# Decode attention over a key/value cache: the order of key and value loads and of the scores and values products within a slot

## The chip, the cores and the metric

The kernel runs on one core of one Trainium2 chip. The metric is the device time of one execution in microseconds: the median of three runs. A profile of one further execution gives the span from its first to its last instruction, and what each engine did in between. TensorE multiplies matrices (PE in the profile; its weight loads, PEld, are listed apart), VectorE (DVE), ScalarE (ACT) and GpSimd (POOL) do the rest, and SyncE (SP) issues the loads. On-chip data lie in SBUF, the results of products in PSUM.

## What is computed

One decoding step for 8 sequences: a layer norm, attention of 32 query heads over a cache of 8 key/value heads with 8192 positions of 128 elements each, and beside it a small token-mixing block, summed with the input.

```python
B, D, Hq, Hkv, Sk, Dh, F = 8, 512, 32, 8, 8192, 128, 1792
xn = _layernorm(x)                                   # x: (B, 1, D)
q = (xn @ wq).reshape(B, 1, Hq, Dh).transpose(0, 2, 1, 3)
k = repeat(k_cache, Hq // Hkv, axis=1)               # cache: (B, Hkv, Sk, Dh)
v = repeat(v_cache, Hq // Hkv, axis=1)
p = softmax(einsum("bhqd,bhkd->bhqk", q, k) * Dh ** -0.5)
o = einsum("bhqk,bhkd->bhqd", p, v)
a = o.transpose(0, 2, 1, 3).reshape(B, 1, Hq * Dh) @ wo
h = _layernorm(xn)
u = gelu(einsum("bsd,sf->bdf", h, w1) + b1)
y = (einsum("bdf,fs->bds", u, w2) + b2).transpose(0, 2, 1)
return x + a + y
```

All of it is float32. The two caches hold 64 pairs (sequence, key/value head) with 4 MB of keys and 4 MB of values each; with the weights that makes 553.69 MB to be read.

## The kernel before

The work is cut into 64 **slots**, one for each pair (sequence, key/value head), numbered by `s`. `slot` (L365) is called for slots 0 and 1 ahead of a loop, for slots 2 to 61 in a loop of four slots a turn (L408), and for 62 and 63 behind it. There are two buffers for keys, `K[0]` and `K[1]`, and two for values, `V[0]` and `V[1]`; pair `s` uses number `k = s % 2`. The order of the instructions on each engine is written by hand: an engine runs its own in the order of the code, and semaphores hold it where data are missing.

A slot of the kernel before does this, for pair `s` with its keys in `K[k]`:

- DVE transposes the keys in place in four quarters (`turn`, L238), and between the first and the second the probabilities of pair `s - 1`, which lie in PSUM (`sm_turn`, L267).
- PE multiplies the probabilities of pair `s - 1` with its values (`pv`, L274, 16 products for a pair, which the profile counts as 32), sums their denominators (`o_sums`, L295), ends the mixing block's step of the slot before (`mx_end`, L341) and begins a new one (`mx_begin`, L325).
- SP issues the load of the values of pair `s + 1` into `V[1 - k]`, where those of `s - 1` lay.
- PE makes the scores of pair `s` (`qk`, L244, as many products as `pv`); then SP issues the load of the keys of pair `s + 2` into `K[k]`.
- DVE picks the results of pair `s - 1` out of PSUM (`o_pick`, L279 to L282), PE places them (`o_place`, L285).
- ACT and POOL do the mixing block's step (`mx_steps`, L329 to L337), DVE prepares the queries and the mixing block's data of the next slot (`q_place`, `mx_pick`) and adds the mixing block's result (`y_add`, L306).
- Softmax: DVE takes the maximum (`sm_max`, L250); one product spreads it over the partitions and DVE makes the bias of it (`sm_bias`, L254 to L256); ACT takes the exponential (`sm_exp`, L259); DVE scales the results of pair `s - 1` (`o_norm`, L298 to L300); PE brings the probabilities into the order that the next slot's `sm_turn` needs (`sm_place`, L263, the placing product).

All loads of keys, values and the output weights go through SP's queue, in the order of the code. The loop is made with `iteration_sync="staggered"`: each of its four slots is a stage, and the semaphores of a stage are set back while the loop goes on. Line L408 is where the engines' events for that stand. In the code, the calls of `tc.previous_stage_wait` put the point at which PE, DVE, ACT and POOL report the stage before as finished inside the slot; there is none for SP.

Behind slot 63 come the values product of the last pair, its results (`o_last`, L288 to L291), the regrouping of all results (`regroup`, L420 to L422: the first seven sequences ahead of that values product, the last one behind it), and the product with the output weights: 24 of its 32 tiles into one PSUM tile (L436), which is copied out and folded (L439 to L442), and the last eight tiles straight into the sum (L445). `load_wo` (L80) brings these weights into `K[0]` and `K[1]` once the last keys are used, the second half in pieces of 8, 4, 3 and 1 tiles. L446 copies the sum, L447 writes the output.

Of the kernel before, what the change touches and what calls it, by code (L numbers as in the profile page):

```python
# [14 lines left out]
B, D, HQ, HKV, SK, DH, F = 8, 512, 32, 8, 8192, 128, 1792  # L15
REP = HQ // HKV
P = 128
NT = SK // P
Q = 32
NB = P // Q  # L20
NG = NT // 16
NU = NT // NG
BS = Q // B
# [5 lines left out]
N_IT = B * HKV  # L29
NW = 24  # L30
# [4 lines left out]
def attn_mixer_kernel(ctx: ExitStack, tc: tile.TileContext, x, kc, vc, wq, wo, w1, b1, w2, b2, out):  # L35
    nc = tc.nc
# [12 lines left out]
    def misc():  # L49
        turns[0] += 1  # L50
        return MI[turns[0] % 2]
# [5 lines left out]
    V = [ring.tile([P, NT, DH], F32, name=f"v{k}") for k in range(2)]  # L57
# [8 lines left out]
    def load(to, src, n, pieces=(NT,)):  # L66
        rows = src.rearrange("b h (p t) d -> (b h) p t d", p=P)[n]
        at = 0
        for w in pieces:
            nc.sync.dma_start(to[:, at:at + w, :], rows[:, at:at + w, :])  # L70
            at += w
# [4 lines left out]
    def load_wo(a, pieces):  # L76
        rows = wo.rearrange("(p a c) n -> a p c n", p=P, a=2)[a]
        at = 0
        for w in pieces:
            nc.sync.dma_start(WO[a][:, at:at + w, :], rows[:, at:at + w, :])  # L80
            at += w
# [13 lines left out]
    quarter = [slice(j * D // NB, (j + 1) * D // NB) for j in range(NB)]  # L95
# [34 lines left out]
    fold = const.tile([P, Q], F32, name="fold")  # L130
# [19 lines left out]
    OX = const.tile([P, N_IT, REP, NB], F32, name="ox")  # L150
# [14 lines left out]
    xo = const.tile([P, 32, Q], F32, name="xo")  # L165
    nc.vector.memset(xo, 0.0)
    wide = const.tile([P, D], F32, name="wide")
# [4 lines left out]
    O = [ps_o.tile([P, 512], F32, name=f"o{k}") for k in range(2)]  # L172

    MH = ps_h.tile([P, 512], F32, name="mh")
    MI = [ps_m.tile([P, 512], F32, name=f"misc{k}") for k in range(3)]
# [60 lines left out]
    def turn(k, a, w=NT // 4):  # L236
        t = K[k][:, a:a + w, :].rearrange("p t d -> p (t d)")
        nc.vector.transpose(t, t)  # L238

    def qk(k):  # L240
        kt = K[k].rearrange("p (u g) d -> p g u d", g=NG)
        for j in range(NB):
            for g in range(NG):
                nc.tensor.matmul(S[k][g * Q:(g + 1) * Q, :], W[k][:, j, :], kt[:, g, :, j * Q:(j + 1) * Q],  # L244
                                 start=(j == 0), stop=(j == NB - 1))
# [3 lines left out]
    def sm_max(k):  # L249
        nc.vector.tensor_reduce(MR, S[k], AX.X, ALU.max)  # L250
# [7 lines left out]
    def sm_exp(k):  # L258
        nc.scalar.activation(PR[k], S[k], AF.Exp, bias=NBIAS, scale=SCALE, accum_out=LR[:, k:k + 1])  # L259

    def sm_place(k):
        m = misc()
        nc.tensor.matmul(m, perm, PR[k], start=True, stop=True)  # L263
        return m

    def sm_turn(k, m):
        nc.vector.transpose(PT[k], m)  # L267
# [3 lines left out]
    def pv(k, u0=0, u1=NU):  # L271
        for u in range(u0, u1):
            c = u % NB
            nc.tensor.matmul(O[k][c * Q:(c + 1) * Q, :], PT[k][:, u * Q:(u + 1) * Q],  # L274
                             V[k][:, u * NG:(u + 1) * NG, :].rearrange("p t d -> p (t d)"),
                             start=(u < NB), stop=(u >= NU - NB))

    def o_pick(k):
        nc.vector.tensor_tensor(OM.rearrange("p (g d) -> p g d", g=NG), O[k].rearrange("p (g d) -> p g d", g=NG),  # L279
                                dm.unsqueeze(2).to_broadcast([P, NG, DH]), ALU.mult)  # L280
        nc.vector.tensor_add(OB, OM[:, :256], OM[:, 256:])
        nc.vector.tensor_add(OB[:, :DH], OB[:, :DH], OB[:, DH:])  # L282

    def o_place(k):
        nc.tensor.matmul(MH[:, k * REP:(k + 1) * REP], OB[:, :DH], sel, start=True, stop=True)  # L285

    def o_last(k):
        nc.vector.tensor_copy(OM[:, :256], O[k][:, :256])  # L288
        nc.scalar.copy(OM[:, 256:], O[k][:, 256:])
        for g in range(NG):  # L290
            nc.tensor.matmul(MH[:, k * REP:(k + 1) * REP], OM[:, g * DH:(g + 1) * DH], selg[:, g, :],  # L291
                             start=(g == 0), stop=(g == NG - 1))

    def o_sums(k):
        nc.tensor.matmul(MH[:, 64 + k * REP:64 + (k + 1) * REP], LR[:, k:k + 1].to_broadcast([P, P]), sel, start=True, stop=True)  # L295

    def o_norm(k, s):
        nc.vector.reciprocal(RD, MH[:, 64 + k * REP:64 + (k + 1) * REP])  # L298
        nc.vector.tensor_tensor(OS, MH[:, k * REP:(k + 1) * REP], RD, ALU.mult)  # L299
        nc.vector.tensor_tensor(OX[:, s], OS.unsqueeze(2).to_broadcast([P, REP, NB]),  # L300
                                block.unsqueeze(1).to_broadcast([P, REP, NB]), ALU.mult)

    proj, mixed = MH[:, P:2 * P], MH[:, 2 * P:3 * P]

    def y_add():
        nc.vector.tensor_add(yacc, mixed, yacc)  # L306
# [17 lines left out]
    def mx_begin(k):  # L324
        nc.tensor.matmul(MI[2][:FP, :], BM[k].to_broadcast([B, FP]), hn, start=True, stop=True)  # L325

    def mx_steps(k, loop):
        for j in range(NF // HKV):
            nc.scalar.activation(G, MI[2][:FP, :], AF.Gelu_apprx_tanh, bias=MW[k][:, 1, j:j + 1], scale=MW[k][:, 0, j:j + 1])  # L329
            if loop and not j:  # L330
                tc.previous_stage_wait(nc.scalar.engine)
            nc.gpsimd.tensor_tensor(G if j else ACC, G, MW[k][:, 2, j:j + 1].to_broadcast([FP, D]), ALU.mult)  # L332
            if loop and not j:
                tc.previous_stage_wait(nc.gpsimd.engine)
            if j:
                nc.gpsimd.tensor_add(ACC, ACC, G)  # L336
        nc.scalar.activation(sink, epst[:1], AF.Exp)  # L337

    def mx_end(k):
        for j in range(NB):  # L340
            nc.tensor.matmul(mixed[j * Q:(j + 1) * Q, :], BW[k], ACC[:, quarter[j]], start=True, stop=True)  # L341
# [5 lines left out]
    m = misc()  # L347
# [14 lines left out]

    def slot(s, k, placed, left=2, loop=False):  # L365

        if placed is not None:
            turn(k, 0)
            sm_turn(1 - k, placed)
            for a in range(1, 4):  # L370
                turn(k, a * quart)
            pv(1 - k)
            o_sums(1 - k)
            mx_end(1 - k)
        mx_begin(k)
        if loop:
            tc.previous_stage_wait(nc.tensor.engine)
        if left:
            load(V[1 - k], vc, s + 1)
        qk(k)  # L380
        if left > 1:
            load(K[k], kc, s + 2)
        elif left:
            load_wo(0, (NT // REP,))
        else:
            load_wo(1, (NW - 16, 4, 3, 1))
        if placed is not None:
            o_pick(1 - k)
            o_place(1 - k)
        mx_steps(k, loop)  # L390
        if left:
            q_place(s + 1, 1 - k)
            mx_pick(1 - k, s + 1)
        if placed is not None:
            y_add()
        if loop:
            tc.previous_stage_wait(nc.vector.engine)
        sm_max(k)
        sm_bias()
        sm_exp(k)  # L400
        if placed is not None:
            o_norm(1 - k, s - 1)
        return sm_place(k)

    tc.prologue_barrier()
    m = slot(0, 0, None)
    m = slot(1, 1, m)
    with tc.For_i(2, N_IT - 2, 4, iteration_sync="staggered") as s:  # L408
        for n in range(4):
            m = slot(s + n, n % 2, m, loop=True)  # L410
            if n < 3:
                tc.stage_boundary()
    m = slot(N_IT - 2, 0, m, left=1)
    m = slot(N_IT - 1, 1, m, left=0)

    def regroup(b0, b1, copy):
        for b in range(b0, b1):
            nc.tensor.matmul(O[0][:, b * Q:(b + 1) * Q], OX[:, b * HKV:(b + 1) * HKV].rearrange("p h r j -> p (h r j)"), fold,  # L420
                             start=True, stop=True)
        copy(xo.rearrange("p c (b s) -> p c b s", s=BS)[:, :, b0:b1, 0],  # L422
             O[0][:, b0 * Q:b1 * Q].rearrange("p (b c) -> p c b", c=Q))

    sm_turn(1, m)
    regroup(0, B - 1, nc.scalar.copy)
    pv(1)
    o_sums(1)
    mx_end(1)
    o_last(1)  # L430
    o_norm(1, N_IT - 1)
    regroup(B - 1, B, nc.vector.tensor_copy)
    y_add()
    for c in range(NW):
# [3 lines left out]
        nc.tensor.matmul(proj[j * Q:(j + 1) * Q, :], gather[:, j].rearrange("p b s -> p (b s)"), yacc, start=True, stop=False)  # L438
    nc.vector.tensor_copy(wide[:, :256], S[0][:, :256])  # L439
    nc.scalar.copy(wide[:, 256:], S[0][:, 256:])  # L440
    for j in range(NB):
        nc.tensor.matmul(proj[j * Q:(j + 1) * Q, :], fold, wide[:, quarter[j]], start=False, stop=False)  # L442
    for c in range(NW, 32):
        for j in range(NB):
            nc.tensor.matmul(proj[j * Q:(j + 1) * Q, :], xo[:, c, :], WO[1][:, c - 16, quarter[j]], start=False, stop=(c == 31))  # L445
    nc.vector.tensor_copy(yacc, proj)  # L446
# [29 lines left out]
```

## Time and profile before

| | us |
|---|---|
| median of 3 runs (lowest, highest) | 1298.01 (1297.66, 1300.28) |
| the profiled execution's own time | 1300.48 |
| its span | 1298.7 |
| busy: PE, DVE, ACT, POOL | 905.7, 857.5, 331.3, 218.0 |
| mean granted TensorE clock | 0.769 |
| read from memory | 553.69 MB, 426 GB/s over the span |

In the rows that follow, a line such as "604.03 0.33 SPq L70" of the timeline gives the start, the duration, the engine and the line of the kernel, then what was written from what; in square brackets stands how long the engine had been idle and what ended that. A row of a group of instructions gives the busy time of all of them and the mean duration of one in ns, then the idle time before them and what ended most of it. An engine's name with a q behind it is its sequencer: what it does there is not counted as busy. Rows of stretches give, for each stretch of time, the busy time (and the number) of PE, PEld, DVE, ACT and POOL, then the granted clock of TensorE as a share of full speed, the busy share of the DMA engines, and GB/s.

### The profile page before, as it was taken

How to read it: one execution, taken by the hardware profiler on the slowest of the kernel's cores; microseconds unless marked ns; L12 is line 12 of the kernel's file. 1: busy time of each engine (PE TensorE's matmuls, PEld its weight loads, DVE VectorE, ACT ScalarE, POOL GpSimd, SP SyncE). 2: the span in 40 equal slices, each digit the busy share in tenths (PEclk: the TensorE clock that was granted, in tenths of full speed). 3: DMA queues.
4: the chain of work that ended last, by engine and by line, in shares of the span. 5: the costliest groups of instructions: out<-in, count | busy, mean ns of one | idle time of the engine just before them, and what ended most of it. 6: DMA issues, size and time to landing. Idle time of an engine off the chain costs nothing.

```text
span 1298.7 us, 15589 instructions
## 1 busy us (share of the span) xinstructions
PE 905.7 (70%) x5498; PEld 271.0 (21%) x5498; DVE 857.5 (66%) x1261; ACT 331.3 (26%) x458; POOL 218.0 (17%) x205
## 2 busy tenths in 40 slices
PE   4657767767767767766766766776766776776777
PEld 1112212212212212212212211221221221211223
DVE  3666766766766776776776776776676676676671
ACT  1223123223223223223223213213213312312321
POOL 1112122122112112112112112112112212212211
PEclk9678778778768778768777777867777877877877
DMA  9999999999999999999999999999999999999994
GB/s 405 435 433 426 432 435 436 436 432 428 432 436 436 435 432 428 433 436 436 434 432 428 434 436 436 434 432 428 434 436 436 433 429 432 434 436 436 433 427 196
DMA packets 19789, 553.84 MB, mean 426 GB/s; under 512 B 2332, under 2 KB 2364, under 8 KB 2628
## 3 DMA queue, kind: packets, MB, share of 16 engines
q1 hardware_dynamic: 19620, 553.67, 98.8%
q8 instruction: 7, 0.11, 0.0%
q0 software_dynamic: 160, 0.04, 0.0%
q14 instruction: 2, 0.02, 0.0%
HBM read 553.69 MB, written 0.02 MB: 426 GB/s over the span
## 4 chain that ended last, share of the span: by engine, by line
PE 58%; DVE 20%; issue 15%; DMA 6%; DVEq 1%; POOL 0%; ACT 0%; POOLq 0%
PE o L274 28%; PE s L244 17%; DVE k L238 8%; PE misc L325 5%; DMA k<-in_A_k_cache_dram 4%; DVE mr L250 3%; DVE pt L267 3%; DMA v<-in_A_v_cache_dram 3%; PE misc L254 2%; PE mh L341 2%; PE mh L285 2%; PE mh L295 2%; DVE sq L255 1%; DVE nb L256 1%; DVE os L299 1%
## 5 line engine op out<-in xcount | busy, mean ns | idle before, releaser
L238 DVE STREAM_TRANSPOSE k<-k 128x2048 f32<-128x2048 f32 x256 | 574.0, 2280 | 154.5 <-issue 131.2
L274 PE MATMUL o<-v,pt 128*32 128x512 f32 x2048 | 370.3, 889 | 193.3 <-DVE pt L267 191.8
L329 ACT ACT_TABLE_LOAD x64 | 82.1, 1283 | 799.0 <-PE misc L325 787.7
L244 PE MATMUL s<-k,w 128*32 128x512 f32 x2048 | 234.6, 599 | 0.0
L332 POOL TENSOR_TENSOR macc<-g,mw 112x512 f32<-112x512 f32 x64 | 66.7, 1042 | 989.4 <-ACT g L329 989.4
L274 PEld LDWEIGHTS o<-v,pt 128*32 128x32 f32 x2048 | 87.0, 155 | 504.4 <-issue 359.2
L263 PE MATMUL misc<-pr,perm 128*128 128x512 f32 x128 | 116.3, 1006 | 105.6 <-ACT pr L259 105.6
L306 DVE TENSOR_TENSOR yacc<-mh,yacc 128x128 f32<-128x128 f32 x64 | 18.7, 292 | 188.2 <-PE mh L285 188.2
L329 ACT ACTIVATE g<-misc,mw 112x512 f32<-112x512 f32 x128 | 99.5, 777 | 79.3 <-POOL macc L332 77.8
L244 PEld LDWEIGHTS s<-k,w 128*32 128x32 f32 x2048 | 60.2, 110 | 166.4 <-issue 140.9
L337 ACT ACT_TABLE_LOAD x64 | 82.1, 1283 | 1.1
L336 POOL TENSOR_TENSOR macc<-macc,g 112x512 f32<-112x512 f32 x64 | 80.8, 1263 | 5.1
L332 POOL TENSOR_TENSOR g<-g,mw 112x512 f32<-112x512 f32 x64 | 66.6, 1040 | 56.9 <-ACT g L329 56.9
L254 PE MATMUL misc<-nident,mr 128*128 128x128 f32 x128 | 31.2, 326 | 62.7 <-DVE mr L250 62.7
L325 PE MATMUL misc<-hn,bm 8*112 8x512 f32 x128 | 71.7, 640 | 0.6 <-DVE mw L315 0.6
L259 ACT ACTIVATE pr<-s,nb 128x512 f32<-128x512 f32 x64 | 44.0, 687 | 35.1 <-DVE rd L298 23.9
L263 PEld LDWEIGHTS misc<-pr,perm 128*128 128x128 f32 x128 | 25.8, 252 | 117.8 <-ACT pr L259 115.9
L250 DVE TENSOR_REDUCE mr<-s 128x1 f32<-128x512 f32 x64 | 43.6, 681 | 6.6 <-PE s L244 6.6
L267 DVE STREAM_TRANSPOSE pt<-misc 128x512 f32<-128x512 f32 x64 | 43.2, 675 | 2.5 <-PE misc L263 2.5
L279 DVE TENSOR_TENSOR om<-o,dm 128x512 f32<-128x512 f32 x63 | 41.7, 662 | 2.5 <-PE o L274 2.1
L255 DVE TENSOR_TENSOR sq<-misc,hmask 128x128 f32<-128x128 f32 x64 | 18.7, 292 | 37.1 <-PE misc L254 37.1
L254 PEld LDWEIGHTS misc<-nident,mr 128*128 128x128 f32 x128 | 19.0, 187 | 69.1 <-DVE mr L250 69.1
(98 smaller groups left out, 378.3 us busy)
## 6 DMA issues: line engine op xcount, KB each, us to landing
v<-in_A_v_cache_dram SPq DMA_DIRECT2D x64, 4096.0 KB, 19.8
k<-in_A_k_cache_dram SPq DMA_DIRECT2D x63, 4096.0 KB, 24.2
v<-in_A_wq_dram SPq DMA_DIRECT2D x2, 4096.0 KB, 17.0
k<-in_A_k_cache_dram SPq DMA_DIRECT2D x2, 2048.0 KB, 30.3
k<-in_A_wo_dram SPq DMA_DIRECT2D x1, 4096.0 KB, 25.2
k<-in_A_wo_dram SPq DMA_DIRECT2D x1, 2048.0 KB, 10.1
k<-in_A_wo_dram SPq DMA_DIRECT2D x1, 1024.0 KB, 12.2
k<-in_A_wo_dram SPq DMA_DIRECT2D x1, 768.0 KB, 13.5
```

The source lines that it names most:

```text
L238: nc.vector.transpose(t, t)
L244: nc.tensor.matmul(S[k][g * Q:(g + 1) * Q, :], W[k][:, j, :], kt[:, g, :, j * Q:(j + 1) * Q], start=(j == 0), stop=(j == NB - 1))
L250: nc.vector.tensor_reduce(MR, S[k], AX.X, ALU.max)
L254: nc.tensor.matmul(m[:, :P], MR.to_broadcast([P, P]), nident, start=True, stop=True)
L263: nc.tensor.matmul(m, perm, PR[k], start=True, stop=True)
L267: nc.vector.transpose(PT[k], m)
L274: nc.tensor.matmul(O[k][c * Q:(c + 1) * Q, :], PT[k][:, u * Q:(u + 1) * Q], V[k][:, u * NG:(u + 1) * NG, :].rearrange("p t d -> p (t d)"), ...
L325: nc.tensor.matmul(MI[2][:FP, :], BM[k].to_broadcast([B, FP]), hn, start=True, stop=True)
L329: nc.scalar.activation(G, MI[2][:FP, :], AF.Gelu_apprx_tanh, bias=MW[k][:, 1, j:j + 1], scale=MW[k][:, 0, j:j + 1])
L332: nc.gpsimd.tensor_tensor(G if j else ACC, G, MW[k][:, 2, j:j + 1].to_broadcast([FP, D]), ALU.mult)
L336: nc.gpsimd.tensor_add(ACC, ACC, G)
L337: nc.scalar.activation(sink, epst[:1], AF.Exp)
```

## The change

In each slot, SP issues the load of the keys of pair `s + 2` ahead of that of the values of pair `s + 1`; the latter moves to the end of the slot. The scores of pair `s` are made ahead of the values product of pair `s - 1`. That product runs in two halves, one ahead of the placing product of pair `s` and one behind it. Sums, pick, placing and scaling of the results (`o_sums`, `o_pick`, `o_place`, `o_norm`) are those of pair `s - 2` now, so they are a slot later; a new argument `n` of `slot` (0, 1, 2) leaves out in the first two slots what has no pair yet. In the last slot the regrouping of the first seven sequences moves ahead of the scores and into another PSUM tile (`MI[0]`). Behind the last slot the results of pairs 62 and 63 are done one after the other, and the fold products stand behind four of the eight last tiles.

```diff
--- before.py
+++ after.py
@@ -362,72 +362,84 @@
 
 
 
-    def slot(s, k, placed, left=2, loop=False):
-
-        if placed is not None:
+    def slot(s, k, placed, n, left=2, loop=False):
+
+        if n:
             turn(k, 0)
             sm_turn(1 - k, placed)
             for a in range(1, 4):
                 turn(k, a * quart)
-            pv(1 - k)
-            o_sums(1 - k)
+        if n > 1:
+            o_sums(k)
+        if n:
             mx_end(1 - k)
         mx_begin(k)
         if loop:
             tc.previous_stage_wait(nc.tensor.engine)
-        if left:
-            load(V[1 - k], vc, s + 1)
+        if not left:
+            regroup(0, B - 1, nc.scalar.copy)
         qk(k)
         if left > 1:
             load(K[k], kc, s + 2)
-        elif left:
-            load_wo(0, (NT // REP,))
-        else:
+        elif not left:
             load_wo(1, (NW - 16, 4, 3, 1))
-        if placed is not None:
-            o_pick(1 - k)
-            o_place(1 - k)
+        if n > 1:
+            o_pick(k)
+            o_place(k)
         mx_steps(k, loop)
         if left:
             q_place(s + 1, 1 - k)
             mx_pick(1 - k, s + 1)
-        if placed is not None:
+        if n:
             y_add()
         if loop:
             tc.previous_stage_wait(nc.vector.engine)
         sm_max(k)
         sm_bias()
         sm_exp(k)
-        if placed is not None:
-            o_norm(1 - k, s - 1)
-        return sm_place(k)
+        if n:
+            pv(1 - k, 0, NU // 2)
+        if n > 1:
+            o_norm(k, s - 2)
+        m = sm_place(k)
+        if n:
+            pv(1 - k, NU // 2, NU)
+        if left:
+            load(V[1 - k], vc, s + 1)
+        if left == 1:
+            load_wo(0, (NT // REP,))
+        return m
+
+    def regroup(b0, b1, copy):
+        for b in range(b0, b1):
+            nc.tensor.matmul(MI[0][:, b * Q:(b + 1) * Q], OX[:, b * HKV:(b + 1) * HKV].rearrange("p h r j -> p (h r j)"), fold,
+                             start=True, stop=True)
+        copy(xo.rearrange("p c (b s) -> p c b s", s=BS)[:, :, b0:b1, 0],
+             MI[0][:, b0 * Q:b1 * Q].rearrange("p (b c) -> p c b", c=Q))
 
     tc.prologue_barrier()
-    m = slot(0, 0, None)
-    m = slot(1, 1, m)
+    m = slot(0, 0, None, 0)
+    m = slot(1, 1, m, 1)
     with tc.For_i(2, N_IT - 2, 4, iteration_sync="staggered") as s:
         for n in range(4):
-            m = slot(s + n, n % 2, m, loop=True)
+            m = slot(s + n, n % 2, m, 2, loop=True)
             if n < 3:
                 tc.stage_boundary()
-    m = slot(N_IT - 2, 0, m, left=1)
-    m = slot(N_IT - 1, 1, m, left=0)
-
-
-
-    def regroup(b0, b1, copy):
-        for b in range(b0, b1):
-            nc.tensor.matmul(O[0][:, b * Q:(b + 1) * Q], OX[:, b * HKV:(b + 1) * HKV].rearrange("p h r j -> p (h r j)"), fold,
-                             start=True, stop=True)
-        copy(xo.rearrange("p c (b s) -> p c b s", s=BS)[:, :, b0:b1, 0],
-             O[0][:, b0 * Q:b1 * Q].rearrange("p (b c) -> p c b", c=Q))
+    m = slot(N_IT - 2, 0, m, 2, left=1)
+    m = slot(N_IT - 1, 1, m, 2, left=0)
+
+
 
     sm_turn(1, m)
-    regroup(0, B - 1, nc.scalar.copy)
-    pv(1)
+    pv(1, 0, NU // 2)
+    o_pick(0)
+    o_place(0)
+    o_sums(0)
+    o_norm(0, N_IT - 2)
+    pv(1, NU // 2, NU)
     o_sums(1)
+    o_last(1)
     mx_end(1)
-    o_last(1)
     o_norm(1, N_IT - 1)
     regroup(B - 1, B, nc.vector.tensor_copy)
     y_add()
@@ -438,9 +450,10 @@
         nc.tensor.matmul(proj[j * Q:(j + 1) * Q, :], gather[:, j].rearrange("p b s -> p (b s)"), yacc, start=True, stop=False)
     nc.vector.tensor_copy(wide[:, :256], S[0][:, :256])
     nc.scalar.copy(wide[:, 256:], S[0][:, 256:])
-    for j in range(NB):
-        nc.tensor.matmul(proj[j * Q:(j + 1) * Q, :], fold, wide[:, quarter[j]], start=False, stop=False)
     for c in range(NW, 32):
+        if c == NW + 4:
+            for j in range(NB):
+                nc.tensor.matmul(proj[j * Q:(j + 1) * Q, :], fold, wide[:, quarter[j]], start=False, stop=False)
         for j in range(NB):
             nc.tensor.matmul(proj[j * Q:(j + 1) * Q, :], xo[:, c, :], WO[1][:, c - 16, quarter[j]], start=False, stop=(c == 31))
     nc.vector.tensor_copy(yacc, proj)
```

## The prediction

> **What bounds the kernel now.** First the page's head and its queue table, then the busy time by stretches of the loop and of the end.
>
> ```profile
> span 1298.7 us, 15589 instructions
> ...
> q1 hardware_dynamic: 19620, 553.67, 98.8%
> ```
> ```profile
> 91.90:1234.40 1142.50, 807.33 (x4839) 236.71 (x4838) 780.48 (x1121) 300.99 (x413) 197.36 (x177) 0.76 1.00 433
> ```
> ```profile
> 1280.00:1284.00 4.00, 3.86 (x34) 1.82 (x26) 0.53 (x2) 0.37 (x1) 0.00 (x0) 0.83 0.36 146
> ```
>
> The one load queue fills 98.8% of the span, and its share is 1.00 in the loop (the columns are PE, PEld, DVE, ACT, POOL, clock, DMA share, GB/s). Loads end near 1281.4 (0.36 of the 4 us after 1280). So the loop is bound by the transfers, and 17 us of tail follow. One slot in order of time:
>
> ```profile
> 595.54 2.31 DVE L238 STREAM_TRANSPOSE k<-k 128x2048 f32<-128x2048 f32 x1 [1.53 <-issue]
> ...
> 598.37 6.66 DVE L238 STREAM_TRANSPOSE k<-k 128x2048 f32<-128x2048 f32 x3
> ```
> ```profile
> 604.03 0.33 SPq L70 DMA_DIRECT2D v<-in_A_v_cache_dram  x1
> ...
> 605.52 3.64 PE L244 MATMUL s<-k,w 128*32 128x512 f32 x32
> ...
> 609.30 0.33 SPq L70 DMA_DIRECT2D k<-in_A_k_cache_dram  x1
> ...
> 609.72 0.68 DVE L250 TENSOR_REDUCE mr<-s 128x1 f32<-128x512 f32 x1
> ...
> 609.83 1.04 POOL L332 TENSOR_TENSOR g<-g,mw 112x512 f32<-112x512 f32 x1 [0.89 <-ACT g L329]
> ...
> 610.46 0.49 PE L254 MATMUL misc<-nident,mr 128*128 128x128 f32 x2 [0.98 <-DVE mr L250]
> ...
> 611.77 0.69 ACT L259 ACTIVATE pr<-s,nb 128x512 f32<-128x512 f32 x1 [0.50 <-DVE rd L298]
> ...
> 612.60 2.07 PE L263 MATMUL misc<-pr,perm 128*128 128x512 f32 x2 [1.66 <-ACT pr L259]
> 615.02 2.31 DVE L238 STREAM_TRANSPOSE k<-k 128x2048 f32<-128x2048 f32 x1 [2.78 <-issue]
> ...
> 618.08 5.83 PE L274 MATMUL o<-v,pt 128*32 128x512 f32 x32 [3.40 <-DVE pt L267]
> ```
>
> Compute is done before the slot is over: DVE idles 2.78 us before the next transposes. What ends that idleness matters most here. The events of the loop line L408, and the wait of SP's queue on it:
>
> ```profile
> L408 POOLq EVENT_SEMAPHORE  x2: 17/17/17, 614.7 to 614.7; - x2
> L408 DVEq EVENT_SEMAPHORE  x2: 21/21/21, 614.7 to 614.8; - x2
> L408 PEldq EVENT_SEMAPHORE  x2: 51/51/51, 614.7 to 614.8; - x2
> ...
> L408 POOLq COMPARE_BRANCH  x1: 49/49/49, 611.0 to 611.0; - x1
> ...
> L408 SPq EVENT_SEMAPHORE  x1: 28/28/28, 614.6 to 614.6; - x1
> ```
> ```profile
> SPq L408 <- DMA k<-in_A_k_cache_dram: 263.1, 59, 5.4
> ```
>
> POOL had branched to the next slot at 611.0, yet it, DVE and PE all pass L408 only at 614.7, just after SP's event at 614.6. SP stands there, 59 times, until a K load lands. I read it so: **at each slot boundary every engine waits for SP**, and SP gives that release after the last load it issues in the slot, once the loads of the slot before have landed. Now the last issue (K, 609.30) comes 5 us before the landing, so only the landing counts: one slot lasts two transfers.
>
> ```profile
> 91.92 2.31 DVE L238 STREAM_TRANSPOSE k<-k 128x2048 f32<-128x2048 f32 x1 [2.26 <-DMA k<-in_A_k_cache_dram]
> ```
> ```profile
> 1234.47 2.31 DVE L238 STREAM_TRANSPOSE k<-k 128x2048 f32<-128x2048 f32 x1 [1.82 <-issue]
> ```
>
> From slot 3 to slot 62 are 59 slots in 1142.55 us, 19.37 each.
>
> **The change, part by part.** *SP.* K for pair s+2 is issued first (it waits for the scores, as now), then V for s+1, which waits for the second half of the values product, now PE's last work in the slot. Nothing follows it on SP but the release, and behind that stand all four other engines. So the next slot can't begin before the chain transposes, scores, softmax, half, placing product, half, V issue, release has run through; the early key load buys nothing inside the loop, as DVE may not touch the keys before the release. Slots no longer overlap, and the chain is the period:
>
> - release to first transpose 0.2 (estimate from 614.6/614.7 against 615.02, half of that in the slots without a branch); four transposes with the turn of the probabilities between, 595.54 to 605.03: 9.49; to PE 0.1. The results' pick and placing no longer wait for a product of their own slot; DVE does the pick under the scores, as now.
> - scores. They take the place at which the values product now starts after idle time:
>
> ```profile
> L274 PE MATMUL o<-v,pt 128*32 128x512 f32 x2048 | 370.3, 889 | 193.3 <-DVE pt L267 191.8
> ...
> L244 PE MATMUL s<-k,w 128*32 128x512 f32 x2048 | 234.6, 599 | 0.0
> ```
> ```profile
> 47.82 0.69 DVE L250 TENSOR_REDUCE mr<-s 128x1 f32<-128x512 f32 x1 [6.64 <-PE s L244]
> ...
> 50.63 1.12 PE L263 MATMUL misc<-pr,perm 128*128 128x512 f32 x2 [1.58 <-ACT pr L259]
> ```
> ```profile
> 53.33 6.61 PE o L274 x32
> ```
> ```profile
> 609.20:612.50 3.30, 0.77 (x4) 0.48 (x4) 1.90 (x7) 2.77 (x5) 2.30 (x2) 0.97 0.87 377
> 612.50:615.00 2.50, 2.07 (x2) 0.50 (x2) 0.00 (x0) 0.05 (x1) 0.00 (x0) 0.50 1.03 446
> ...
> 618.10:621.00 2.90, 2.90 (x16) 0.87 (x20) 2.90 (x2) 0.00 (x0) 0.00 (x0) 0.50 0.89 384
> ```
>
>   Both products have the same shapes and count; the one at the head of PE's burst takes 370.3/64 = 5.79 us, the one behind it 234.6/64 = 3.67, and the granted clock is 0.50 at the burst's start. After the change PE has only small products at the slot's head and then waits until the transposes end, 9.7 after the release. So scores: 5.79, and the values 3.64 in all (ends: 3.64, and 6.61, the dearest cold one in the chain of waits).
> - end of scores (609.16) to end of the bias product (610.95): 1.79. Then half the values 1.82, under which bias, exponential and normalization lie (the exponential ends at 612.46, 3.3 after the scores; the half ends 3.6 after). Placing product at full clock 1.12, second half 1.82.
> - to SP 0.15 (the K issue at 609.30 follows the scores' end, 609.16, by 0.14), issue 0.33, release 0.1.
>
> Sum 0.2 + 9.49 + 0.1 + 5.79 + 1.79 + 1.82 + 1.12 + 1.82 + 0.15 + 0.33 + 0.1 = **22.7 us a slot**, 3.34 above now. Two transfers take 19.37, so the loads land in time, and the queue stands empty some 3 us a slot. With all at full clock the sum is 20.55; with scores at 6.6, 23.5.
>
> *Mixer.* Its start no longer waits for the values product, so ACT and POOL run beside the transposes.
>
> ```profile
> L332 POOL TENSOR_TENSOR macc<-g,mw 112x512 f32<-112x512 f32 x64 | 66.7, 1042 | 989.4 <-ACT g L329 989.4
> ...
> L336 POOL TENSOR_TENSOR macc<-macc,g 112x512 f32<-112x512 f32 x64 | 80.8, 1263 | 5.1
> ```
>
> No row shows POOL beside a transpose. Bounds: nothing to all of POOL's 1.04 + 1.04 + 1.26 = 3.3 us added to the chain. The nearest: the reduction at 609.72 with POOL running from 609.83 took 0.68, the one at 47.82 with POOL idle 0.69. So I take nothing.
>
> *Head.* K for pair 2 is issued behind the same scores as now; slot 1's values come after its scores, yet their V is issued before the queue is empty. Slot 3 waits for as many bytes as now: no change.
>
> *Tail.* Counted from slot 62's release (about 1234.3 now, so 64.4 to the end). After the change V for 63 is issued at about 22.3. The queue is empty by then, so a startup is paid:
>
> ```profile
> 0.75 0.86 SPq L63 DMA_DIRECT2D v<-in_A_wq_dram  x2
> ```
> ```profile
> 22.78 3.64 PE L207 MATMUL s<-v,sq 128*32 128x512 f32 x32 [2.95 <-DMA v<-in_A_wq_dram]
> ```
>
> Two transfers took 22.0 from an idle queue, 2.7 over 19.37. Three transfers (V, both halves of Wo): 22.3 + 2.7 + 29.1 = 54.1. Pair 63 is barely ahead of that (estimates from the terms above): no release stands behind slot 62, so DVE begins its keys at 18.7; transposes to 28.2, scores to 34, halves and placing of pair 62 to 40.5, the values of 63 to 44.5, its result some 3 later, and then the projection of 24 tiles to 54:
>
> ```profile
> 1285.39 6.70 PE L436 MATMUL s<-k,xo 128*32 128x512 f32 x48 [0.37 <-DVE xo L422]
> ```
>
> Regrouping of the first seven batches (moved under the last transposes) and the fold product (moved past four tiles) leave the path. Behind the last byte:
>
> ```profile
> L445 PE MATMUL mh<-k,xo 128*32 128x128 f32 x64 | 2.1, 273 | 0.0
> ```
> ```profile
> 1295.26 0.29 DVE L446 COPY yacc<-mh 128x128 f32<-128x128 f32 x1 [2.67 <-PE mh L445]
> ```
>
> half of the last 2.1, the copy, and 3.15 to the span's end: 4.5. The tail is 58.6, 5.8 less than now (ends: nothing, and the 12 of the first rival).
>
> Total: 1298.7 + 59 x 3.34 - 5.8 = 1490 of span. The profiled run took 1300.48 for its span of 1298.7, and the median of the runs is 1298.01, 0.7 under that span. Forecast: **1489 us**.
>
> **Rivals.**
>
> 1. *Faster, transfers stay the bound.* If engines can enter the next slot without SP's last issue, the queue stays full, the last byte lands near 1281.4 and 4.5 follow: 1286, 1285 by the median. For it: DVE's own work to the normalization is below 19.37. Against: POOL waiting from 611.0 to 614.7. It decides where the second half ends under 19.37 - 0.6 after the release. 0.07.
> 2. *Slower, but the scores run at full clock* (PE's small products keep it up): 20.55 a slot, 1292.2 + 59 x 1.18 = 1362. Against: the 0.50 rows after a shorter idle time. The Trainium skill, "TensorE: Matmul & The Clock Gate", Part 1, says to model the warm-up as under 1% of a span; by that the scores cost about the same anywhere, and this would be the time. The trace differs: 2.1 us in each of 64 slots, a tenth of the span. 0.04.
> 3. *Slower still*: the clock falls again in the gap after the scores, as it has by 612.5, so that halves and placing run at half rate: 2 x 1.5 + 0.95 more, 26.65 a slot, 1292.2 + 59 x 7.28 = 1722; or POOL takes its 3.3 from the transposes, 26.0 a slot, 1684. Against: the first half now fills that gap. 0.09 in all, partial cases included.
>
> **How the numbers follow.** The forecast has 0.80. 21.8 to 24.1 a slot (PE's phase against its clock, a little of rival 3) gives 1436 to 1572, which holds nearly all of it and some of rival 3: about 8 in 10. A measurement of this kernel tells 0.2% from no change, 2.6 us. Only rival 1 is faster, 0.07; no change needs a slot of 19.4 to 19.5, 0.01; slower 0.92.
>
> **What would show it.** Right: transposes of successive slots start 22.7 apart; SP waits on L70 for the values product and hardly on L408; DMA share in the loop about 0.85 and some 370 GB/s; scores near 5.8 a slot, values near 3.7; L408 events of all engines right behind the V issue. Wrong: a DMA share of 1.00 and slots of 19.4 (rival 1); scores at 3.7 (rival 2); transposes above 2.31 or a clock of 0.50 under the halves (rival 3). The sum falls with the reading of L408 alone: if the release doesn't hang on the V issue, the change gains 1%.

## The result, and the profile after

| | before | after |
|---|---|---|
| median of the runs, us (lowest, highest; runs) | 1299.06 (1297.66, 1300.28; 4) | 1513.37 (1512.55, 1513.92; 4) |
| span of the profiled execution, us (its own time) | 1298.7 (1300.48) | 1511.3 (1513.12) |
| mean granted clock | 0.769 | 0.747 |

The ratio is 1.165, with an interval of 1.1629 to 1.167: the change makes the kernel slower by a sixth. The forecast of 1489 us is 24 us (1.6%) too low, and the time lies in the range.

First the page of the kernel after: its head, the load queue (packets, MB, share of the span), and the shares of the chain that ended last.

```profile
span 1511.3 us, 15580 instructions
...
q1 hardware_dynamic: 19620, 553.67, 87.5%
...
DVE 44%; PE 31%; issue 22%; DMA 2%; DVEq 1%; SPq 0%; ACT 0%; ACTq 0%
```

The same bytes now fill 87.5% of the span and not 98.8%, and transfers are 2% of the chain. DVE and PE take turns instead. Nearly the whole loop, from slot 3 on (columns as before: PE, PEld, DVE, ACT, POOL, clock, DMA share, GB/s):

```profile
91.90:1448.50 1356.60, 786.26 (x4829) 226.67 (x4822) 778.72 (x1121) 300.92 (x413) 197.31 (x177) 0.74 0.87 365
```

The queue moved 365 GB/s where it moved 433 before. One slot of the kernel after, in order of time:

```profile
599.61 2.31 DVE L238 STREAM_TRANSPOSE k<-k 128x2048 f32<-128x2048 f32 x1 [4.26 <-issue]
...
609.15 6.03 PE L244 MATMUL s<-k,w 128*32 128x512 f32 x32 [7.74 <-DVE k L238]
...
615.33 0.33 SPq L70 DMA_DIRECT2D k<-in_A_k_cache_dram  x1
...
616.89 1.92 PE L274 MATMUL o<-v,pt 128*32 128x512 f32 x16
...
618.75 1.12 PE L263 MATMUL misc<-pr,perm 128*128 128x512 f32 x2
...
619.80 1.92 PE L274 MATMUL o<-v,pt 128*32 128x512 f32 x16
...
621.86 0.33 SPq L70 DMA_DIRECT2D v<-in_A_v_cache_dram  x1
622.64 2.31 DVE L238 STREAM_TRANSPOSE k<-k 128x2048 f32<-128x2048 f32 x1 [4.39 <-issue]
```

Nothing of one slot lies beside the next: the transposes at 622.64 begin 0.78 after the V issue, and the slot is 23.03 long, in a chain without a hole. (The four slots of a turn differ: 23.03, 23.5, 23.7 and 21.9, in this order again and again; their mean is 23.04.) The events of the loop line, L423 in the new numbering, at the end of this slot:

```profile
L423 ACTq EVENT_SEMAPHORE  x2: 17/17/17, 622.3 to 622.4; - x2
L423 POOLq EVENT_SEMAPHORE  x2: 17/17/17, 622.3 to 622.4; - x2
L423 DVEq EVENT_SEMAPHORE  x2: 21/21/21, 622.3 to 622.4; - x2
L423 PEldq EVENT_SEMAPHORE  x2: 51/51/51, 622.3 to 622.5; - x2
...
L423 SPq EVENT_SEMAPHORE  x1: 27/27/27, 622.2 to 622.2; - x1
```

SP's event comes at 622.2, right behind its V issue, and the other four engines pass at 622.3. The waits of SP's queue (engine, line, waited for: total, times, longest):

```profile
SPq L70 <- PE s L244: 489.1, 32, 16.3
SPq L70 <- PE o L274: 388.3, 62, 22.2
```

The 59 waits of the loop line on a landing, 263.1 us before, are gone from the list; on L70, 62 waits on the values product stand where 32 did (287.1 us). The groups of the kernel after that answer to those of before:

```profile
L238 DVE STREAM_TRANSPOSE k<-k 128x2048 f32<-128x2048 f32 x256 | 573.9, 2280 | 275.8 <-issue 261.8
L244 PE MATMUL s<-k,w 128*32 128x512 f32 x2048 | 383.8, 918 | 475.6 <-DVE k L238 475.6
L274 PE MATMUL o<-v,pt 128*32 128x512 f32 x2048 | 246.1, 598 | 0.0
```

The two products have changed places, and with it the price: scores 383.8/64 = 6.00 us a slot (3.67 before), values 246.1/64 = 3.85 (5.79 before).

**Where the time went.** The first transposes of slot 3 start at 93.49 (91.92 before), those of slot 62 at 1451.96: 59 slots of 23.03 against 19.37. So 1298.7 + 1.6 (head) + 59 x 3.66 (loop) - 4.9 (tail: 59.3 behind slot 62's first transposes, 64.2 before) = 1511.3.

### The profile page after: what moved, and what is told of

The parts are those of the page before. It is cut to its first block, busy times and chain, and to the rows that moved or that the text cites. A ratio compares the mean times of both kernels' runs of the same rounds, so it can differ in the third digit from the quotient of the medians.

```text
span 1511.3 us, 15580 instructions
## 1 busy us (share of the span) xinstructions
PE 884.4 (59%) x5498; PEld 259.2 (17%) x5498; DVE 857.5 (57%) x1261; ACT 331.2 (22%) x458; POOL 218.0 (14%) x205
## 3 DMA queue, kind: packets, MB, share of 16 engines
q1 hardware_dynamic: 19620, 553.67, 87.5%
## 4 chain that ended last, share of the span: by engine, by line
DVE 44%; PE 31%; issue 22%; DMA 2%; DVEq 1%; SPq 0%; ACT 0%; ACTq 0%
DVE k L238 35%; PE s L244 25%; DVE pt L267 3%; DVE mr L250 2%; PE misc L254 2%; DMA k<-in_A_k_cache_dram 2%; PE mh L285 1%; DVE sq L255 1%; DVE nb L256 1%; PE o L274 1%; DVE os L299 1%; DVE ox L300 1%; DVE rd L298 1%; PE s L448 0%; PE misc L263 0%
## 5 line engine op out<-in xcount | busy, mean ns | idle before, releaser
L238 DVE STREAM_TRANSPOSE k<-k 128x2048 f32<-128x2048 f32 x256 | 573.9, 2280 | 275.8 <-issue 261.8
L244 PE MATMUL s<-k,w 128*32 128x512 f32 x2048 | 383.8, 918 | 475.6 <-DVE k L238 475.6
L274 PE MATMUL o<-v,pt 128*32 128x512 f32 x2048 | 246.1, 598 | 0.0
L244 PEld LDWEIGHTS s<-k,w 128*32 128x32 f32 x2048 | 89.4, 159 | 761.3 <-issue 486.3
L336 POOL TENSOR_TENSOR macc<-macc,g 112x512 f32<-112x512 f32 x64 | 81.1, 1267 | 5.1
L274 PEld LDWEIGHTS o<-v,pt 128*32 128x32 f32 x2048 | 53.5, 109 | 132.6 <-issue 125.0
L325 PE MATMUL misc<-hn,bm 8*112 8x512 f32 x128 | 75.6, 670 | 0.6 <-DVE mw L315 0.6
L263 PE MATMUL misc<-pr,perm 128*128 128x512 f32 x128 | 73.0, 652 | 1.6 <-ACT pr L259 1.6
L295 PE MATMUL mh<-sel,lr 128*128 128x4 f32 x128 | 22.8, 249 | 57.7 <-issue 50.1
L250 DVE TENSOR_REDUCE mr<-s 128x1 f32<-128x512 f32 x64 | 43.6, 681 | 11.9 <-PE s L244 11.9
L295 PEld LDWEIGHTS mh<-sel,lr 128*128 128x128 f32 x128 | 19.0, 187 | 113.0 <-issue 84.3
```

## The experiments

Each ratio is to the kernel before on the same chip. Theory A is that of the prediction: the loop's release, which all engines wait for, hangs on SP's last issue. Its rivals were that the order of the loads, or of the products, costs the time by itself.

### SP reports early

Kernel after, with SP's report for the release put right behind the key load:

```diff
         if left > 1:
             load(K[k], kc, s + 2)
+            if loop:
+                tc.previous_stage_wait(nc.sync.engine)
```

> One line is added to the changed kernel: SP, too, reports the slot before as finished inside the slot, between its load of keys and its load of values. Nothing is left out of the computation. Theory (the release of the next slot hangs on SP's last issue, the V load): the release then comes when the values of the slot before have landed, the queue stays full, slots go back to 19.4 us (now 23.0), and the time is 1294 us, 1290 to 1298: 59 slots of 19.4 and the 59.3 us that the changed kernel takes from the release of slot 62 to its end. Rival A (the slots are serial because of the data, keys to scores to values, whoever reports): 1513 stays, slots of 23.0. Rival B (the queue runs dry because keys and values are asked for too late): slots well over 19.4, 1350 and more, with a DMA share under 0.95 in the loop.

Measured: 1330.57 us (1326.39 to 1334.34), ratio 1.0251 [1.0234, 1.0267]. One line takes 183 of the 214 us away, with every product and load in the changed order. Theory A holds for most of it; 36 us more than I expected are left. SP's wait at the loop line (L425 here), and the loop's middle:

```profile
SPq L425 <- DMA v<-in_A_v_cache_dram: 220.1, 59, 7.9
```
```profile
120.00:1200.00 1080.00, 707.57 (x4448) 206.23 (x4452) 738.32 (x1034) 275.64 (x378) 181.52 (x162) 0.80 0.99 421
```

The release now hangs on a landing again, as before, but the queue moves 421 GB/s, at a busy share of 0.99. The next rows show how late the keys are asked for.

```profile
187.14 0.33 SPq L70 DMA_DIRECT2D k<-in_A_k_cache_dram  x1
...
193.70 0.33 SPq L70 DMA_DIRECT2D v<-in_A_v_cache_dram  x1
```

The values issued before it had landed when SP passed the loop line at 189.9, 2.8 us after the K issue; the next V landing let it pass at 211.3, so these two transfers took 21.4 and not 19.4. In the kernel before, the shortest such lead is that of the values, 10.6 us (issued 604.03, when only the keys that landed at 614.6 were still on the way). That the short lead costs the rate fits these numbers; no run changed it alone, so it is not shown.

### Only the order of the loads

Kernel before, with the key load issued ahead of the value load:

```diff
-        if left:
-            load(V[1 - k], vc, s + 1)
         qk(k)
         if left > 1:
             load(K[k], kc, s + 2)
+        if left:
+            load(V[1 - k], vc, s + 1)
...
```

> The kernel before, with the K load ahead of the V load on SP and nothing else changed: scores still follow the values product. Theory: the V load waits for nothing that comes late, SP's last issue stays 5 us ahead of the landing, slots stay at 19.4 and the time within 0.4% of before: 1294 to 1300 us. Rival (the order of the two loads itself costs, since the next slot then waits for the values and no longer for the keys): slower than 1310 us.

Measured: 1299.68 us, ratio 1.0007 [0.9995, 1.0018]. The order of the loads costs nothing by itself. The release hangs on the other landing now, and SP waits for it about as long (263.1 before):

```profile
SPq L410 <- DMA v<-in_A_v_cache_dram: 234.9, 59, 7.8
```

### The values product in one piece

Kernel after, with the whole product ahead of the placing product:

```diff
-            pv(1 - k, 0, NU // 2)
+            pv(1 - k)
...
-        if n:
-            pv(1 - k, NU // 2, NU)
         if left:
             load(V[1 - k], vc, s + 1)
```

> The changed kernel with the values product in one piece ahead of the placing product. Theory: the placing product (1.12 us) leaves the stretch ahead of the V issue, so each slot is 1.05 us shorter: 22.0 us, 59 times, 1451 us (1445 to 1460). Rival (the placing product or the exponential is what the next slot waits for): the same or slower, 1513 us and more.

Measured: 1413.54 us, ratio 1.0877 [1.0861, 1.0894]; 99.8 us less than after, 1.7 a slot where I had 1.05; the time lies below the range that I had given. The sign and the place are as expected: the V issue comes earlier by the placing product, which no longer stands between the halves. Most of the surplus is in the scores:

```profile
L244 PE MATMUL s<-k,w 128*32 128x512 f32 x2048 | 352.7, 852 | 480.8 <-DVE k L238 480.8
```

352.7/64 = 5.51 us against 6.00: 0.5 a slot from a product that the edit doesn't touch. What sets it is taken up below.

### PE kept busy ahead of the scores

Kernel after, with six more products of the same shape while PE waits for the transposes, into the tile that the scores then overwrite:

```diff
         if loop:
+            for _ in range(6):
+                nc.tensor.matmul(S[k], ident, rj.rearrange("p j i d -> p (j i d)"), start=True, stop=True)
             tc.previous_stage_wait(nc.tensor.engine)
```

> The changed kernel with six products of 128x128 by 128x512 added in each loop slot, behind the mixer's start and ahead of the scores, into the scores' own tile, which the scores overwrite. They fill the time in which PE waits for the transposes. Theory (the scores run at the head of PE's burst at half clock): scores fall from 6.0 us to 3.7 to 4.2, slots to 20.7 to 21.2 us, and the time to 1375 to 1410 us. Rival (the scores are slow for another reason than the clock, or the added products come late and delay them): scores stay at 6 us, 1513 us or more.

Measured: 1385.55 us, ratio 1.0657 [1.064, 1.0674]. More work makes the kernel 128 us faster than after, 2.2 a slot, and the scores' row says where:

```profile
L244 PE MATMUL s<-k,w 128*32 128x512 f32 x2048 | 255.0, 642 | 113.8 <-DVE k L238 113.8
```

255.0/64 = 3.98 a slot, near the 3.64 of a product at full clock, and the mean granted clock is 0.941 where it was 0.747. So the half-rate start of the scores is real, and while the release hangs on the V issue, it is worth 128 of the 214 us. The 183 of SP's report are not to be added to it: they come from taking the whole chain off the path, slow scores included. The prediction's second rival, 1362 with no slow start at all, is 24 below this; some slots still paid, at 5.3.

### Both together, and the output weights earlier

SP's early report and four of those filling products:

> The changed kernel with SP's report between its two loads (as in e1_sp_reports, 1330.6 us) and four of the filling products of e4_kept_busy. Theory (in e1 the release no longer hangs on the V load, but the K load, asked for at the end of cold scores, comes so late that the queue runs thin, 421 GB/s in place of 433): warm scores end 2 us earlier, the K load with them, and the loop is bound by the transfers again: slots of 19.4 us, 433 GB/s in the loop, 1294 us (1290 to 1299). Rival (slots with a release by landed values cost about 0.5 us whatever the scores do): 1320 us and more.

Measured: 1309.23 us (1302.75 to 1315.11), ratio 1.0083 [1.0057, 1.0108]. 21 us less than with the report alone, 15 above what I expected: the scores take 305.4/64 = 4.77 us, so four products don't keep the clock up in every slot, and single slots of 20 to 21.8 are scattered between others, mostly of 19.2 to 19.6. The middle of its loop:

```profile
120.00:1200.00 1080.00, 869.52 (x4973) 284.68 (x4975) 737.50 (x1053) 281.30 (x387) 185.97 (x167) 0.93 1.00 429
```

The same with the first half of the output weights issued behind the scores of slot 62, ahead of the values of 63:

```diff
         if left > 1:
             load(K[k], kc, s + 2)
...
-        elif not left:
+        elif left:
+            load_wo(0, (NT // REP,))
+        else:
             load_wo(1, (NW - 16, 4, 3, 1))
...
-        if left == 1:
-            load_wo(0, (NT // REP,))
```

> As e5_reports_and_busy, and in slot 62 the first half of the output weights is loaded ahead of the values of pair 63, right behind the scores. Theory (behind the loop the queue stands empty until the values product of pair 61 ends): the last byte lands some 6 us earlier, the tail is then bound by pair 63's own work, and 2 to 3 us go: 1292 us (1287 to 1297). Rival (values of 63 are late now): slower than e5.

Measured: 1313.84 us (1298.76 to 1323.77), ratio 1.0112 [1.0097, 1.0127]. The runs lie 25 us apart, far more than the 2 to 3 us that I expected to gain; the gain isn't seen, nothing more follows, and the scatter is unexplained.

### Steps or a sum

Why did the scores change in the one-piece kernel? The score products of four slots in a row, of the kernel after:

```profile
240.54 6.01 PE L244 MATMUL s<-k,w 128*32 128x512 f32 x32 [7.76 <-DVE k L238]
...
263.68 6.38 PE L244 MATMUL s<-k,w 128*32 128x512 f32 x32 [7.58 <-DVE k L238]
...
287.16 6.59 PE L244 MATMUL s<-k,w 128*32 128x512 f32 x32 [7.83 <-DVE k L238]
...
310.74 5.05 PE L244 MATMUL s<-k,w 128*32 128x512 f32 x32 [7.74 <-DVE k L238]
```

If a product takes 3.64 at full clock and starts at half of it, a duration d means that the clock turned 2 x (d - 3.64) after the start. The granted clock itself shows the first of these turns where the working puts it:

```profile
240.60:245.20 4.60, 4.60 (x24) 1.13 (x28) 1.68 (x7) 0.00 (x0) 0.00 (x0) 0.50 0.79 342
245.30:246.50 1.20, 1.20 (x13) 0.14 (x5) 0.00 (x0) 0.00 (x0) 0.00 (x0) 0.97 0.00 0
```

The turns are at 245.28, 269.16, 293.06 and 313.56: 23.88, 23.90 and 20.50 apart, which is 7.00, 7.00 and 6.01 times 3.4133 us, a sixth of the 20.48 of the next sentence. In the one-piece kernel the four turns from 255.71 on are 20.48, 20.48 and 20.49 apart, 6.00 each, and the next comes after 7.00. So the clock turns at the edges of a time grid that the kernel doesn't set, and a score product's price depends on its phase to it. The Trainium skill, "TensorE: Matmul & The Clock Gate", Part 1, gives such a window, 4096 cycles at 1.2 GHz, free-running; the trace agrees with its 3413 ns.

A chain that waits for the turn in each slot can then only last whole windows, in the mean over a few slots. Four slots in a row last 92.17 us after, 27.0 windows, and 85.33 us in the one-piece kernel, 25.0. With PE kept busy, where most scores run at full clock and wait for no turn, four in a row can last 82.67, 24.2 windows. To test it, the maximum L250 (0.68 us, on the chain) is taken twice, and then, between the two, once more over a quarter of the row (0.28 us):

```diff
         sm_max(k)
+        nc.vector.tensor_reduce(MR, S[k][:, :128], AX.X, ALU.max)
+        sm_max(k)
```

(the second added line alone is the kernel "twice", both are "twice and a quarter")

> The changed kernel with the maximum of the scores taken twice (0.68 us more on the chain of each slot). Theory of steps (the scores end at a fixed time after an edge of PE's clock windows of 3.413 us, so the slots lock to whole windows: four slots are 92.2 us, 27.0 windows, in the changed kernel and 85.3, 25.0, in e3_one_piece): slots lock to 7 windows each, 23.89 us, all alike, and the time is 1564 us (1560 to 1568). Rival (costs simply add): 0.65 a slot, 59 times, 1552 us, and the four lengths of a slot stay apart.

> As e7_max_twice, and between the two a maximum over a quarter of the scores (0.28 us more on the chain). Theory of steps: the slots stay at 7 windows, 23.89 us, and the time is that of e7 within 3 us. Rival (costs add): 17 us above e7.

Measured: 1569.63 us and 1574.00 us, ratios 1.2086 [1.2067, 1.2105] and 1.2121 [1.21, 1.2142]. The first step costs 56 us, more than 64 x 0.68 = 44; the second 4.4, where 64 x 0.28 gives 18. In the loop that second difference is smaller still: from the transposes of the probabilities in slot 3 to those in slot 62 it is 1409.96 (95.67 to 1505.63) and 1410.6 (98.34 to 1508.93), 23.90 and 23.91 a slot, 7.00 windows each. Costs on this chain come in steps here. Two things didn't follow. Both times lie a little above what I had given, by 1.6 and 1.4 us. And in "twice" the slots were not alike (22.8 to 25.4): its values product started at half rate in some of them (at 613.33 the first half took 3.32 in place of 1.92, at a granted clock of 0.50 up to 615.50).

```profile
L274 PE MATMUL o<-v,pt 128*32 128x512 f32 x2048 | 275.3, 661 | 0.0
```

That is 275.3/64 = 4.30 a slot against 3.85 after. In "twice and a quarter" the row is

```profile
L274 PE MATMUL o<-v,pt 128*32 128x512 f32 x2048 | 256.7, 621 | 0.0
```

or 4.01, 0.29 less: as much as the quarter's maximum adds (292 ns). So the added work was paid for by less time at half rate, and the period stayed. That the period is what is fixed, and PE's slow time what gives way, is how I read it; the whole windows of all four kernels bear it out, but no run sets the phase.

### The changed order without a release

Kernel after, with the loop written out (no stages, so no releases; the barriers ahead of the loop and at the end are dropped):

```diff
-    with tc.For_i(2, N_IT - 2, 4, iteration_sync="staggered") as s:
-        for n in range(4):
-            m = slot(s + n, n % 2, m, 2, loop=True)
-            if n < 3:
-                tc.stage_boundary()
+    for s in range(2, N_IT - 2):
+        m = slot(s, s % 2, m, 2)
```

> The changed kernel with the loop written out: all 64 slots in the changed order, no stages, no releases, nothing else changed. Theory: SP's late V load holds nothing but the queue itself, which is full by then; slots of 19.4 us bound by the transfers, last byte near 1281, some 6 us behind it: 1289 us (1285 to 1297). Rival A (the changed order is serial by its data): 1513 stays. Rival B (the queue runs thin in this order, as in e1_sp_reports): 1310 to 1330. Rival C (fetching 15,000 instructions that were a loop costs time): above 1297, with PE or DVE idle on issue.

Measured: 1295.77 us (1295.63 to 1296.85), ratio 0.997 [0.9958, 0.9981]. With the one-line report of SP, this is the run that settles theory A: loads, products and results stand in the order of the change, and the time is 217.6 us lower. SP's wait on the values product, what DVE waits for, the scores, and the middle of the loop:

```profile
SPq L70 <- PE o L274: 384.4, 62, 11.6
```
```profile
DVE k L238 <- DMA k<-in_A_k_cache_dram: 83.2, 59, 13.8
```
```profile
L244 PE MATMUL s<-k,w 128*32 128x512 f32 x2048 | 367.2, 883 | 338.7 <-DVE k L238 338.7
```
```profile
120.00:1200.00 1080.00, 723.54 (x4558) 206.37 (x4558) 755.41 (x1055) 283.33 (x389) 186.21 (x166) 0.81 1.00 432
```

SP waits for the second half as often and as long as after (384.4 against 388.3 us, 62 times), and the scores are nearly as slow (5.74 a slot). Neither costs anything, because nobody stands behind SP any more:

```profile
608.87 2.31 DVE L238 STREAM_TRANSPOSE k<-k 128x2048 f32<-128x2048 f32 x1 [1.11 <-DMA k<-in_A_k_cache_dram]
...
611.37 0.33 SPq L70 DMA_DIRECT2D v<-in_A_v_cache_dram  x1
```

The next slot's transposes start 2.5 us ahead of the V issue, as soon as the keys land, and the loop is bound by the transfers again.

### The old order in the loop, the changed one behind it

Loads as in the second experiment and the old slot in a loop up to slot 57; slots 58 to 63 in the changed order, written out behind it, with the changed end:

```diff
-    with tc.For_i(2, N_IT - 2, 4, iteration_sync="staggered") as s:
+    with tc.For_i(2, N_IT - 6, 4, iteration_sync="staggered") as s:
...
+    for s in range(N_IT - 6, N_IT - 2):
+        m = slot(s, s % 2, m, 1 if s == N_IT - 6 else 2)
     m = slot(N_IT - 2, 0, m, 2, left=1)
     m = slot(N_IT - 1, 1, m, 2, left=0)
```

> Loop slots as in e2_keys_first (the order before, keys read first, slots of 19.37 us), but the loop ends at slot 57; slots 58 to 63 stand behind it in the changed order, with no release between them. Theory (the changed order is sound, only the release behind the V load makes its slots serial): the six slots run at 17 to 19 us, as slots 62 and 63 of the changed kernel do (18.97 and 17.67 between their turns), pair 63 is done before the last byte has landed, and the tail behind that byte shrinks from 17 to some 6 us: 1290 us (1286 to 1295), faster than before by 0.6%. Rival (the changed order is slower wherever it runs, or the queue runs thin in it): 1298 us or more.

Measured: 1295.68 us (1294.07 to 1298.04), ratio 0.9969 [0.9957, 0.9981]. The changed tail is worth 0.3%, about half of what I expected. The two rows show where the rest may lie:

```profile
1248.13 0.17 DVE L300 TENSOR_TENSOR ox<-os,block 128x16 f32<-128x16 f32 x1
1253.45 2.31 DVE L238 STREAM_TRANSPOSE k<-k 128x2048 f32<-128x2048 f32 x1 [5.15 <-issue]
```

DVE stands still for 5.15 us ahead of the last pair's transposes, so that pair's own work, not the last byte, sets the end. What held it the profile doesn't say ("issue"), and no run was made for it. The keys themselves had probably landed: 16.8 MB were queued behind them and the loads end near 1283.5, which at 433 GB/s puts their landing near 1245 (an estimate). In the gap, between 1250 and 1254, the trace has two small fetches of the program's own instructions (0.01 and 0.02 MB), so a wait for code is a candidate; it is not shown.

These last two kernels are 0.3% faster than the kernel before. That is clear of the noise within their session, but small: the kernel before had a median of 1300.5 there and of 1298.1 and 1298.4 in the others. 553.7 MB at 433 GB/s alone take 1279 us, so little more is to be had.

## Why the prediction was right, and where it was short

**The reading of the loop line was right**, and the whole forecast stood on it. The release comes behind the V issue (events at 622.2 and 622.3). SP reporting earlier takes 183 us away, no release 217.6. Within the kernel after, the two slots behind the loop, which have no release, follow each other in 18.97 and 17.67.

**The sum of a slot** was 22.71 and is 23.03. By its own terms, on the slot shown above:

| step | predicted | measured |
|---|---|---|
| first transpose to scores' start | 9.59 | 9.54 (599.61 to 609.15) |
| scores | 5.79 | 6.03; mean 6.00 |
| scores' end to first half | 1.79 | 1.71 (615.18 to 616.89) |
| first half | 1.82 | 1.86 (to 618.75) |
| placing product | 1.12 | 1.05 (to 619.80) |
| second half to V issue | 1.97 | 2.06 (to 621.86) |
| V issue to next transpose | 0.63 | 0.78 (to 622.64) |

The mis-sized term is above all the scores, 0.24 too low in the slot shown and 0.21 in the mean: I took the mean of the product that stood at that place in the kernel before, but the price there is set by the phase to the clock's grid, and 23.03 a slot is 27 windows in four slots. The second half, the issue and the release add another 0.24, and the other rows take 0.16 back. That the forecast came so near is in part luck: the sum knows no steps, and the one-piece kernel, for which the same terms gave 1451, took 1413.5. At 59 slots the 0.32 is 18.9 us of the miss of 24. The rest: 1.6 in the head, which I had at no change (slot 3 begins 0.66 behind the V issue of slot 2, at 92.83, so it waits for that issue already and not, as I had it, for bytes), 0.9 in the tail (-4.9 and not -5.8), and 2.8 because I set the median 0.7 under the span, as the kernel before had it, while it lies 2.1 above here.

**Signs named ahead.** Transposes 22.7 apart (23.03), SP on L70 for the values product (62 times) and on the loop line no longer for a landing, DMA share 0.85 and 370 GB/s (0.87, 365), values near 3.7 (3.85): all as said.

**Rival 1**, transfers stay the bound, is what this order does when the release is taken away: 1295.8, not the 1285 I had worked out. Its slots are 19.44 in the mean, from slot 3 at 85.54 to slot 62 at 1232.70, and not 19.37 (one of 20.3 in every seven), and the last byte lands near 1287. Why is open; the program that is written out also moves more of its own instructions (0.70 and 0.16 MB where the kernel before moved 0.11 and 0.02).

**Rival 2**, scores at full clock, fell: 6.00 a slot, and 128 us come back when PE is kept busy. The rule of the Trainium skill, "TensorE: Matmul & The Clock Gate", Part 1, that I weighed there, to model the warm-up as under 1% of a typical span, doesn't hold here: these 128 of 1513 us are 8%.

**Rival 3** fell in both parts. POOL now runs beside the transposes (in the slot shown its L336 lies from 606.76 to 608.03, the last two transposes from 604.63 to 609.09), and they take 2280 ns each over the whole execution, as before. The clock stayed up under the halves (1.00 from 616.90 to 618.70 and from 619.80 to 621.70); in the kernel with the second maximum some first halves started at half rate (3.32 in place of 1.92).

## What to carry to other kernels

In a loop with staged releases, look for the engine that reports last and at what its last instruction waits for: that wait is on everyone's path, even on a queue that looks idle. Before moving a load to the end of a slot, let its queue report ahead of it, or write the loop out. Price a product that moves by the clock at its new place, and a serial chain that waits for the clock to rise in each slot in whole steps of the 3.41 us seen here.

## What the runs showed that was not expected

- **Costs in steps.** The loop took 27, 25 and, in the mean, 28 windows of 3.4133 us for four slots (after, one piece, second maximum), and 0.28 us more on the chain of each slot cost 0.6 us in all 59, because the values product spent as much less at half rate.
- **A lower rate at nearly the same busy share.** In the kernel with SP's early report, where the keys were asked for 2.8 us ahead of the queue's end in the slot shown, the loop moved 421 GB/s at a share of 0.99, against 433 at 1.00 in the kernel before, where the lead is 10.6 or more. That the lead is the cause is not shown.
- **Small additions on DVE stretch beside POOL, transposes don't.** From the timelines of the kernel with SP's early report:

```profile
200.78 1.25 DVE L282 TENSOR_TENSOR ob<-ob 128x128 f32<-128x128 f32 x1
```
```profile
200.51 1.36 POOL L336 TENSOR_TENSOR macc<-macc,g 112x512 f32<-112x512 f32 x1
```

L282 adds the two halves of a tile in SBUF and takes 0.29 us in the kernel after with POOL idle (610.16), here 1.25, four times as long. The transposes have one input and kept their 2280 ns. The Trainium skill, "GPSIMD Engine Reference", section 1, Specifications, says that POOL shares its SBUF interfaces with VectorE and that instructions with two SBUF inputs contend; the trace agrees.
